# Moving u loads and out stores into SyncE's queue beside the transposes, and reordering the opening of an attention-and-mixer kernel

## The chip, the cores and the metric

One core of a Trainium2 chip. The metric is device time of one execution in microseconds (us), taken as the median of several runs; spans and stage times come from profiled executions. Engines are named as in the profile: PE is TensorE's matmuls, PEld its weight loads, DVE VectorE, ACT ScalarE, POOL GpSimd, SP SyncE. A "q" behind the name is the engine's instruction queue, where loads and stores are issued. Line numbers such as L351 are lines of the kernel in question; the changed kernel's lines are shifted by some 20.

## The reference

```python
batch, seq, d_model, d_qk, rank = 8, 3136, 256, 64, 32
# gated attention unit
scores = (1 / seq) * z @ z.transpose(0, 2, 1)
x = u * (np.maximum(scores, 0) ** 2 @ v)
# mixer: a low-rank mix over the sequence, then an MLP over the channels
h = x.transpose(0, 2, 1) @ U @ V
y = x + h.transpose(0, 2, 1)
out = y + np.maximum(y @ w_ch1, 0) @ w_ch2        # w_ch1: 256 x 1024, w_ch2: 1024 x 256
```

The score matrix is symmetric. The kernel computes, for each of the 25 tiles of 128 rows, only half of the blocks of its row ("A"), and gets the other half by transposing.

## The kernel before

Four things matter here.

First, PE walks through the 25 output tiles of a batch. For an output tile it needs 12 transposed blocks, a "strip", which SyncE makes from A by one DMA transpose. A strip is ordered 4 output tiles before it is needed (`AHEAD = 4`, 5 buffers).

```python
transpose = nc.sync.dma_start_transpose
pool_dma = nc.gpsimd.dma_start

def turn(b, o):                          # SyncE's queue
    strip = strip_pool.tile([P, HALF, P], BF16, name="strip")
    transpose(out=strip, in_=A[o][:, P:])
    strips[b, o] = strip
```

Second, all plain traffic goes through GpSimd's queue: u in, out back, and v, which is cast from fp32 to bf16 on the way. u and out have two buffers each.

```python
def load_v(b, part):
    ...
        pool_dma(out=v_bf[:, t0:t1, :], in_=rows(v[b])[:, t0:t1, :])
...
def load_u(b, o):
    ...
        pool_dma(out=u_sb[:, :n, :], in_=rows(u[b])[:, t0 : t0 + n, :])
...
                store = pool_dma if b + 1 < B else nc.sync.dma_start
                    store(out=rows(out[b])[:, t : t + nk, :], in_=o_sb[:, :nk, :])
```

Third, the MLP of batch b-1 runs in eight "bursts" between the attention of batch b, and each burst emits one of the nine loads of v of batch b+1 (the last burst two):

```python
burst_at = {4: (0, 1), 8: (2, 3), 13: (4, 5), 17: (6, 7)}
...
    loads = [lambda k=k: load_v(b + 1, V_PARTS[k]) for k in ((n,) if n < NC else (n, n + 1))]
    steps = _merge(steps, loads)
```

v has two buffers, so v of batch b+1 can go in as soon as the attention of batch b-1 has ended, which is at the start of batch b. An engine's queue runs in order, and in GpSimd's queue the v loads stand between stores and u loads.

Fourth, the opening: z of batch 0 is loaded in parts, doubled on VectorE, transposed on PE, and the first four output tiles are computed with scores kept in borrowed room, among it the second v buffer (so v of batch 1 can't come early).

```python
load_z(0, parts[:2]); ...               # GpSimd
double_z(0, parts[:2])                   # VectorE
turn_on_pe([(8, 12), (12, 16)], sets[0])
...
rooms = [v_both[1][:, t : t + 4, :] for t in range(0, NF, 4)]
```

## Time and profile before

| | before |
|---|---|
| median of 3 runs | 1019.78 us (1015.84 to 1021.53) |
| span of the profiled run | 1013.1 us |
| PE busy | 990.8 us (98%) |
| idle PE | 22.3 us |

The page's busy lines, its PE rows in 40 slices, and the chain of work that ended last:

```profile
PE 990.8 (98%) x13816; PEld 785.3 (78%) x13856; DVE 541.2 (53%) x977; ACT 613.5 (61%) x834; POOL 172.2 (17%) x318
...
PE   7899999999999999999999999999999999999998
...
PE 89%; DVE 4%; DMA 3%; ACT 2%; issue 1%; POOL 0%; DVEq 0%; POOLq 0%; ACTq 0%
```

PE is the bound and is full everywhere except in the first slices and the last. The busy times by stretch say where the idle time lies; the columns are the stretch, then busy us and number of instructions of PE, PEld, DVE, ACT and POOL, then granted clock, DMA share and GB/s:

```profile
0.00:30.00 30.00, 21.89 (x258) 16.67 (x259) 17.14 (x33) 20.70 (x30) 12.40 (x28) 1.00 0.79 146
30.00:60.00 30.00, 25.22 (x360) 18.88 (x361) 24.24 (x48) 25.57 (x41) 3.68 (x6) 0.94 1.07 177
60.00:130.00 70.00, 69.95 (x1178) 56.58 (x1174) 50.96 (x95) 51.20 (x73) 14.82 (x25) 1.00 1.17 200
130.00:960.00 830.00, 825.30 (x11676) 660.91 (x11709) 429.29 (x772) 490.96 (x663) 140.73 (x258) 1.00 0.91 168
960.00:1013.10 53.10, 48.47 (x350) 32.26 (x354) 19.58 (x31) 25.10 (x30) 0.55 (x1) 1.00 0.32 92
```

From 60 to 960 PE idles 4.75 us in all.

### The profile page before, as it was taken

The numbers are of one execution on the slowest core, as the hardware profiler recorded it, in microseconds if no ns is written. First come the engines' busy times: TensorE is split into PE (matmuls) and PEld (weight loads), VectorE is DVE, ScalarE is ACT, GpSimd is POOL, SyncE is SP. The second block draws the span as 40 slices with busy tenths as digits, with TensorE's granted clock in tenths as the row PEclk, the third lists the DMA queues.
The fourth block names the chain that finished last, engine by engine and source line by source line (L and its number), as shares of the span: only waits on it lengthen the run. The fifth ranks groups of instructions, "written<-read, shape, count | busy, mean of one in ns | idle before, by whom it ended". The sixth has DMA issues, their size and how long they took to land.

```text
span 1013.1 us, 31291 instructions
## 1 busy us (share of the span) xinstructions
PE 990.8 (98%) x13816; PEld 785.3 (78%) x13856; DVE 541.2 (53%) x977; ACT 613.5 (61%) x834; POOL 172.2 (17%) x318
## 2 busy tenths in 40 slices
PE   7899999999999999999999999999999999999998
PEld 5678878787778877788787887878878788787856
DVE  5878654456544665446644556445664356542242
ACT  6887664667646666456764667556674666643154
POOL 4122112121121111221112211112111120011000
PEclk9999999999999999999999999999999999999999
DMA  8999989999999998989989997989979998778432
GB/s 155 154 199 229 170 155 183 187 177 152 164 193 170 176 168 155 190 168 174 167 170 171 181 169 141 193 170 188 157 154 194 176 179 143 143 136 174 104 97 97
DMA packets 414584, 167.70 MB, mean 166 GB/s; under 512 B 389408, under 2 KB 399328, under 8 KB 414448
## 3 DMA queue, kind: packets, MB, share of 16 engines
q1 hardware_dynamic: 384944, 99.16, 60.7%
q0 software_dynamic: 29504, 66.55, 28.5%
q8 instruction: 108, 1.77, 0.7%
q14 instruction: 28, 0.23, 0.1%
HBM read 61.88 MB, written 25.69 MB: 86 GB/s over the span
## 4 chain that ended last, share of the span: by engine, by line
PE 89%; DVE 4%; DMA 3%; ACT 2%; issue 1%; POOL 0%; DVEq 0%; POOLq 0%; ACTq 0%
PE ps L351 47%; PE ps L562 16%; PE ps L520 16%; PE ps L278 7%; ACT A L291 1%; DMA out_dram<-o_sb 1%; PE ps L385 1%; PE ps L442 1%; DVE A L293 1%; DVE x_bf L502 1%; PE ps L488 1%; DVE both L366 1%; DMA strip<-A 1%; DVE x_bf L375 0%; DMA zT<-z_bf 0%
## 5 line engine op out<-in xcount | busy, mean ns | idle before, releaser
L291 ACT ACTIVATE A<-ps 128x832 bf16<-128x832 f32 (+8 forms) x469 | 352.7, 763 | 155.9 <-PE ps L278 146.0
L351 PE MATMUL ps<-v,A 64*128 64x256 bf16 x4864 | 335.6, 271 | 4.9 <-DVE both L366 2.0
L293 DVE TENSOR_TENSOR A<-A 128x832 bf16<-128x832 bf16 (+8 forms) x469 | 240.3, 524 | 145.7 <-ACT A L291 141.9
L351 PE MATMUL ps<-v,strip 64*128 64x256 bf16 x4420 | 306.8, 269 | 1.3 <-DMA strip<-A 1.2
L351 PEld LDWEIGHTS <-A 64*128 64x128 bf16 x4864 | 239.6, 94 | 49.8 <-issue 15.3
L538 ACT ACTIVATE relu_bf<-ps 128x1024 bf16<-128x1024 f32 (+2 forms) x208 | 187.7, 908 | 142.0 <-PE ps L520 140.0
L351 PEld LDWEIGHTS <-strip 64*128 64x128 bf16 x4420 | 221.3, 94 | 35.5 <-DMA strip<-A 1.7
L562 PE MATMUL ps<-w_bf,relu_bf 128*128 128x256 bf16 x1600 | 204.7, 273 | 0.2 <-ACT relu_bf L536 0.2
L573 DVE TENSOR_TENSOR o_sb<-ps,x_bf 128x512 f32<-128x512 f32 (+1 forms) x104 | 69.7, 670 | 250.8 <-PE ps L562 230.7
L520 PE MATMUL ps<-ut,w_bf 128*128 128x512 bf16 (+2 forms) x856 | 197.3, 351 | 2.5 <-ACT relu_bf L538 0.3
L562 PEld LDWEIGHTS <-relu_bf 128*128 128x128 bf16 x1600 | 155.9, 98 | 47.3 <-issue 3.2
L335 POOL DMA_DIRECT2D u_sb<-in_u_dram x96 | 53.6, 559 | 470.6 <-DVE x_bf L375 438.2
L520 PEld LDWEIGHTS <-w_bf 128*128 128x128 bf16 x896 | 85.1, 98 | 61.3 <-issue 6.8
L278 PE MATMUL ps<-zT 64*128 64x416 bf16 (+8 forms) x812 | 130.7, 312 | 0.0
L365 ACT COPY both<-ps 128x512 f32<-128x512 f32 (+1 forms) x104 | 58.8, 567 | 73.6 <-PE ps L351 66.8
L581 POOL DMA_DIRECT2D out_dram<-o_sb x84 | 46.0, 548 | 274.6 <-DVE o_sb L573 270.6
L366 DVE TENSOR_TENSOR both<-ps,both 128x512 f32<-128x512 f32 (+1 forms) x104 | 69.3, 666 | 27.0 <-ACT both L365 26.7
L375 DVE TENSOR_TENSOR x_bf<-both,u_sb 128x512 bf16<-128x512 f32 (+1 forms) x104 | 69.8, 672 | 3.6
L502 DVE TENSOR_TENSOR x_bf<-ps,x_bf 128x512 bf16<-128x512 f32 (+1 forms) x112 | 65.5, 626 | 8.4 <-PE ps L488 8.2
L278 PEld LDWEIGHTS <-zT 64*128 64x128 bf16 x812 | 42.2, 94 | 4.0
L225 POOL DMA_DIRECT2D v<-in_v_dram x61 | 34.4, 567 | 0.2 <-PE ps L520 0.2
L278 PE MATMUL ps<-relu_bf 64*128 64x416 bf16 (+9 forms) x121 | 23.7, 363 | 2.2 <-ACT A L291 1.0
(52 smaller groups left out, 231.6 us busy)
## 6 DMA issues: line engine op xcount, KB each, us to landing
u_sb<-in_u_dram POOLq DMA_DIRECT2D x96, 256.0 KB, 3.7
out_dram<-o_sb POOLq DMA_DIRECT2D x84, 256.0 KB, 3.3
v<-in_v_dram POOLq DMA_DIRECT2D x57, 192.0 KB, 4.5
strip<-A SPq DMA_TRANSPOSE x196, 5.3
out_dram<-o_sb SPq DMA_DIRECT2D x12, 256.0 KB, 2.1
z_c<-in_z_dram POOLq DMA_DIRECT2D x7, 384.0 KB, 6.3
w_bf<-in_moe_w_ch_dram POOLq DMA_DIRECT2D x2, 512.0 KB, 8.3
u_sb<-in_u_dram POOLq DMA_DIRECT2D x16, 64.0 KB, 2.7
```

The costliest lines, as they stand in the source:

```text
L278: mm(out=ps[:, k, :n], lhsT=zT[halves[k], j, :], rhs=zT_flat[halves[k], c : c + n], start=True, stop=True,)
L291: nc.scalar.activation(out=dst, in_=src, func=AF.Relu, scale=sc)
L293: nc.vector.tensor_tensor(out=dst, in0=dst, in1=dst, op=ALU.mult)
L351: mm(out=acc[t0][h][:, (o - t0) * D : (o - t0 + 1) * D], lhsT=w[halves[h]], rhs=v_both[b % 2][halves[h], j, :], start=start, stop=stop, **kw,)
L365: nc.scalar.copy(out=both[:, :w], in_=banks[1][:, :w])
L366: nc.vector.tensor_tensor(out=both[:, :w], in0=banks[0][:, :w], in1=both[:, :w], op=ALU.add)
L375: nc.vector.tensor_tensor(out=x_at(b, t0, n), in0=split(both[:, :w]), in1=u_sb[:, :n, :].rearrange("p t (a c) -> p t a c", c=P), op=ALU.mult,)
L502: nc.vector.tensor_tensor(out=q, in0=split(ps[h][:, : len(ks) * D]), in1=q, op=ALU.add)
L520: mm(out=ps[i][:, :w] if apart else ps[:, i, :w], lhsT=w1_bf[:, db, (hp + i) * P : (hp + i + 1) * P], rhs=uT[c][:, db, len(chunks[c]) * P ...
L538: nc.scalar.activation(out=relus[c][:, hp : hp + 2, :w], in_=ps[:, :, :w], func=AF.Relu)
L562: mm(out=ps[:, k * D : (k + 1) * D], lhsT=relus[c][:, ht, q : q + P], rhs=w2_bf[:, ht, :], start=(ht == 0), stop=(ht == NH - 1),)
L573: nc.vector.tensor_tensor(out=o_sb[:p, :nk, :].rearrange("p t (a c) -> p t a c", c=P), in0=split(ps[:p, : nk * D]), in1=x_at(b, t, nk)[:p] ...
```

## The change

The intent: take the plain traffic away from GpSimd's software queue and put it in one queue with the transposes; start PE warm and z early; bring all first loads (v, z and weights of batches 0 and 1) up front, with the first strip behind them; hide the first pair closings. The diff, cut to its core:

```diff
+    fifo = nc.sync.dma_start
     transpose = nc.sync.dma_start_transpose
...
+    def first_z(parts):
+        ...
+        nc.vector.memset(wide, 0.0)
+        for _ in range(7):                       # warm PE while z lands
+            mm(out=ps[:, 0, :], lhsT=zT_rest[:, 0, :], rhs=wide, start=True, stop=True)
+        for t0, t1 in parts:                     # z as fp32, by SyncE
+            fifo(out=z_f, in_=rows(z[0])[:, t0:t1, :])
+        for (t0, t1), z_f in zip(parts, landed): # doubled by two engines
+            nc.vector.tensor_copy(out=z_bf[:, t0:t1, 0, :], in_=z_f)
+            nc.scalar.copy(out=z_bf[:, t0:t1, 1, :], in_=z_f)
...
-            pool_dma(out=u_sb[:, :n, :], in_=rows(u[b])[:, t0 : t0 + n, :])
+            fifo(out=u_sb[:, :n, :], in_=rows(u[b])[:, t0 : t0 + n, :])
...
-                store = pool_dma if b + 1 < B else nc.sync.dma_start
-                    store(out=rows(out[b])[:, t : t + nk, :], in_=o_sb[:, :nk, :])
+                    fifo(out=rows(out[b])[:, t : t + nk, :], in_=o_sb[:, :nk, :])
...
-        for s in fetches[:3]:
-            s()
+        run(fetches)
+        if B > 1:
+            for part in V_PARTS:
+                load_v(1, part)
...
-        rooms = [v_both[1][:, t : t + 4, :] for t in range(0, NF, 4)]
+        rooms = [A[j % NT][:, : 2 * NG * P] for j in range(LEAD + NG, LEAD + 3 * NG)]
...
+            if i == 4:
+                for o in outs[::2]:
+                    load_u(0, o)
+                if B > 1:
+                    fifo(out=mark, in_=v_both[1][:1, NF, :8])   # SyncE waits for v of batch 1
...
-        for pair in pairs[-2:]:
+        for o in outs[1::2]:                     # finish and close one output pair at a time
             nxt.pop(0)()
-            use(pair)
-        for o in outs[1::2]:
+            for pair in pairs[-2:]:
+                use(pair, (o - 1, o))
             close_pair(0, o)
...
-                if i in v_at:                    # batch 0's steps
-                    load_v(b + 1, v_at[i])
```

More of the change, by code (lines that the diff above doesn't have):

```diff
@@ L198, in turn_z @@
             )
+    def first_z(parts):
+        z_bf = z_tiles[0] = stage.tile([P, NT, 2, dqk], BF16, name="z_bf")
+        wide = zT_rest[:, :4, :].rearrange("p t c -> p (t c)")
+        nc.vector.memset(wide, 0.0)
+        ps = pair_psum()
+        for _ in range(7):
+            mm(out=ps[:, 0, :], lhsT=zT_rest[:, 0, :], rhs=wide, start=True, stop=True)
+        landed = []
+        for t0, t1 in parts:
+            z_f = u_pool.tile([P, 2, D], FP32, name="u_sb").rearrange("p a c -> p (a c)")
+            z_f = z_f.rearrange("p (t c) -> p t c", c=dqk)
+            fifo(out=z_f, in_=rows(z[0])[:, t0:t1, :])
+            landed.append(z_f)
+        for (t0, t1), z_f in zip(parts, landed):
+            nc.vector.tensor_copy(out=z_bf[:, t0:t1, 0, :], in_=z_f)
+            nc.scalar.copy(out=z_bf[:, t0:t1, 1, :], in_=z_f)
     def turn_on_pe(parts, banks):
@@ L210, in turn_on_pe @@
                 )
-            copy = nc.vector.tensor_copy if t0 % 8 else nc.scalar.copy
+            copy = nc.vector.tensor_copy if t0 % 8 or t1 == NF else nc.scalar.copy
             copy(
@@ L334, in load_u @@
         if o < NF:
-            pool_dma(out=u_sb[:, :n, :], in_=rows(u[b])[:, t0 : t0 + n, :])
+            fifo(out=u_sb[:, :n, :], in_=rows(u[b])[:, t0 : t0 + n, :])
         else:
             for r in halves:
-                pool_dma(out=u_sb[r, 0, :], in_=u[b, NF * P :, :])
+                fifo(out=u_sb[r, 0, :], in_=u[b, NF * P :, :])
         u_tiles[b, t0] = u_sb
@@ L578, in step @@
                 )
-                store = pool_dma if b + 1 < B else nc.sync.dma_start
                 if t < NF:
-                    store(out=rows(out[b])[:, t : t + nk, :], in_=o_sb[:, :nk, :])
+                    fifo(out=rows(out[b])[:, t : t + nk, :], in_=o_sb[:, :nk, :])
                 else:
-                    store(out=out[b, NF * P :, :], in_=o_sb[:TAIL, 0, :])
+                    fifo(out=out[b, NF * P :, :], in_=o_sb[:TAIL, 0, :])
         return [
@@ L608, in start_up @@
         parts = ((8, 16), (0, 8), (16, NF))
-        load_z(0, parts[:2])
+        first_z(parts[:2])
         nc.gpsimd.memset(eye, 1.0)
@@ L624, in start_up @@
             load_v(0, part)
-        double_z(0, parts[:2])
         turn_on_pe([(8, 12), (12, 16)], sets[0])
@@ L632, in start_up @@
             open_pair(0, o)
-            load_u(0, o)
         if B > 1:
             load_z(1, WHOLE)
-        for s in fetches[:3]:
-            s()
+        run(fetches)
+        if B > 1:
+            for part in V_PARTS:
+                load_v(1, part)
         nxt = [s for j in range(LEAD, LEAD + NG) for s in turned(0, j)]
-        rooms = [v_both[1][:, t : t + 4, :] for t in range(0, NF, 4)]
-        rooms = [r.rearrange("p (a t) d -> p a (t d)", a=2) for r in rooms]
-        rooms += [x_bf[:, g].rearrange("p (a w) -> p a w", a=2) for g in (2, 3)]
+        rooms = [A[j % NT][:, : 2 * NG * P] for j in range(LEAD + NG, LEAD + 3 * NG)]
+        rooms = [r.rearrange("p (a w) -> p a w", a=2) for r in rooms]
         pairs = [(8, 9), (10, 11), (12, 13), (14, 15), (6, 7), (3, 4), (5,), (1, 2)]
@@ L644, in start_up @@
         where = {}
+        mark = small.tile([P, D], BF16, name="mark", tag="t1_sb")[:1, :8]
         def make(pair):
@@ L658, in make, with use @@
                 score(0, [(j, c0, NG * P, room) for j in pair])
-        seen = []
-        def use(pair):
+        def use(pair, some):
             for j in pair:
-                for o in outs:
+                for o in some:
                     at = (o - FIRST) * P
-                    stop = [o % 2 == 1 and len(seen) == NT - 1 - h for h in range(2)]
+                    stop = [o % 2 == 1 and j == NF - h for h in range(2)]
                     beside(o, j, where[j][:, at : at + P], stop)
-                seen.append(j)
         for i, pair in enumerate(pairs):
+            if i == 4:
[3 more added lines that the diff above has]
+                    fifo(out=mark, in_=v_both[1][:1, NF, :8])
             if i == 3:
@@ L673, in start_up @@
             if i == 5:
-                ps = pair_psum()
-                turn_on_pe([(16, 20), (20, NF)], [ps[:, 0, :], ps[:, 1, :]])
+                turn_on_pe([(16, NF)], [pair_psum().rearrange("p a w -> p (a w)")])
                 turn_on_pe([(NF, NT)], [pair_psum()[:, 0, :]])
@@ L681, in start_up @@
             if i > 1:
-                use(pairs[i - 2])
-        for pair in pairs[-2:]:
+                use(pairs[i - 2], outs)
+        for o in outs[1::2]:
             nxt.pop(0)()
-            use(pair)
-        for o in outs[1::2]:
+            for pair in pairs[-2:]:
+                use(pair, (o - 1, o))
             close_pair(0, o)
@@ L692, in start_up, with use_stored @@
             load_u(0, o)
-        fetches[3]()
-        if B > 1:
-            double_z(1, WHOLE)
-            turn_z(1, WHOLE)
         pairs = [(j, j - 1) for j in range(LEAD - 1, LEAD - FIRST, -2)]
-        def use_stored(js):
+        def use_stored(js, some):
             for j in js:
-                for o in outs:
+                for o in some:
                     if 0 <= o - j <= HALF:
@@ L712, in start_up @@
         nxt += [lambda pair=pair: make_stored(pair) for pair in pairs[:2]]
-        own = [lambda j=j: use_stored([j]) for j in outs]
-        for s in _merge(nxt, own):
-            s()
+        run(nxt[:2])
+        own = [
+            lambda j=j, some=some: use_stored([j], some)
+            for some in (outs[:2], outs[2:])
+            for j in outs
+            if j <= some[-1]
+        ]
+        run(_merge(nxt[2:], own))
         rest = []
@@ L724, in start_up @@
                 more.pop(0)()
-            use_stored(pair)
+            use_stored(pair, outs)
+            if B > 1 and i in (1, 2):
+                part = ((0, FIRST), (FIRST, NF))[i - 1]
+                double_z(1, (part,))
+                turn_z(1, (part,))
             if i == len(pairs) - 1:
@@ L780 @@
         own = own_at if b else first_at
-        v_at = dict(zip((9, 11, 12, 14, 16, 18, 20, 22, 23), V_PARTS)) if b == 0 else {}
         ahead = dict(zip((2, 3, 6, 7, 10, 11, 14), range(NC)))
```

## The prediction

> **What bounds it now.** TensorE. The page gives PE 990.8 of 1013.1 us busy; the chain of work that ended last is 89% PE. PE idles (windows) 8.1 us in 0-30, 4.8 in 30-60, 0.05 in 60-130, 4.7 in all of 130-960, 4.6 in the tail. In the middle it also runs at its rate: the chain shows 24 attention matmuls in 1.31 us (54.6 ns each) in every batch, one batch per 122.3 us. Steady state has under 5 us to give, the tail is hardly touched; the gain must come from the first 60 us.
>
> **What the opening loses (chain, timeline).**
> 1. PE starts at 4.87: z, issued by GpSimd at 1.30, lands at 4.25 and is doubled by VectorE until 4.82.
> 2. PE is cold: from 4.87 to about 14.5, 16 attention matmuls take 1.71 us against 0.87 later. About 8.5 us at half rate lose 4.2. The granted-clock column shows 1.00. The Trainium skill, "TensorE: Matmul & The Clock Gate", Part 1, says an idle array starts at half clock and needs about 3.4 us of sustained work; the trace agrees in the factor, but took 9 us, with gaps inside.
> 3. From 17 to 29 ScalarE (9.8 of 10 us busy in 20-30) paces the scores.
> 4. From 28.9 to 35.1 the pair closings and an early 1.87 us doubling of batch 1's z stand in PE's way: 2.7 us idle, and half rate again (about 1.5 lost).
> 5. At 46.5 PE waits 1.2 us for a strip queued behind a whole-batch z transpose, at 53 another 1.2 for a square.
>
> **The change.** Seven dummy 512-column matmuls (about 3 us cold) run while z lands; z goes as fp32 by SyncE, cast by VectorE and ScalarE in parallel. Real work starts at 4-4.5 us, warm by 5-6. But ScalarE then binds: it has about 17.6 us of work between 7.3 and 29, so that phase ends near 24.5 instead of 29: items 1-3 together give about 4.5 us. Splitting the last uses by output pair hides closings: about 3. Split, later z transposes: about 1. Against it: 2.1 MB more (w2, v of batch 1) go before the first strip. At the early 220 GB/s they end near 28-30 us; the first strip lands near 33-34, when it is needed: a stall of 0-2 us. Opening total: 7-10 us.
>
> Steady state: 110 loads and 90 stores move from GpSimd to SyncE's queue, 0.33-0.55 us of issue each, off the path. One behind a transpose (1.5 us to issue, 5.3 to landing) lands later, but loads have about a pair and a half of slack, stores two buffers. GpSimd, no longer held by stores and u, will issue the next batch's v in one burst; strips are 4 blocks (about 20 us) ahead. I expect -1 to +2 us.
>
> **Prediction: 1010 us, 1003 to 1017 in 8 of 10.** Faster by over 2%: 0.05; within 2%: 0.92; slower: 0.03.
>
> **What would show it.** First transposes on PE at 4-4.5 us; groups of 16 in 0.87 us by 7 us; second group of outputs starting near 25-26 without a half-rate stretch; PE idle in 0-60 cut from 12.9 to 6-8 us; batch period still 122.3; tail unchanged.
>
> **What would make it wrong.** Strips waiting behind the marker for batch 1's v (a PE stall at 30-40); SyncE blocked in order by a u load or store, giving PE waits in every batch (a longer period); or ScalarE not saturating, so that the warm array gains more.

## More of the kernel before

The timeline of GpSimd at the start of batch 2 shows how v loads (L225) stand among u loads (L335) and stores (L581). The bracket is GpSimd's idle time before the instruction and who ended it:

```profile
246.16 0.55 POOL L335 DMA_DIRECT2D u_sb<-in_u_dram  x1 [6.76 <-DVE x_bf L375]
246.70 0.55 POOL L225 DMA_DIRECT2D v<-in_v_dram  x1
255.05 0.55 POOL L581 DMA_DIRECT2D out_dram<-o_sb  x1 [7.79 <-DVE o_sb L573]
255.59 0.56 POOL L225 DMA_DIRECT2D v<-in_v_dram  x1
```

GpSimd idles most of the time, and each v load goes out only when the store or u load ahead of it has been released by VectorE.

## The result, and the profile after

| | before | after |
|---|---|---|
| median, same chip | 1017.81 us (1014.42 to 1021.53, 4 runs) | 1062.83 us (1060.3 to 1067.68, 4 runs) |
| ratio | | 1.0447 (95%: 1.0391 to 1.0503) |
| span of the profiled run | 1013.1 us | 1061.0 us |
| PE busy / idle | 990.8 / 22.3 us | 1006.9 / 54.1 us |

A ratio is the mean time of one kernel's runs over that of the other's of the same rounds, so it is not quite the ratio of the medians quoted. Executions over 1.5% slower than the fastest of the same kernel are left out of the means. The change is 4.5% slower, where I had put 0.03 on "slower".

The same lines of the page after:

```profile
PE 1006.9 (95%) x13823; PEld 788.5 (74%) x13863; DVE 541.6 (51%) x978; ACT 614.2 (58%) x835; POOL 58.2 (5%) x113
...
PE   7799799997999979999999998999989999999998
...
PE 79%; DMA 13%; DVE 4%; ACT 3%; issue 1%; POOL 0%; SPq 0%; DVEq 0%; ACTq 0%; POOLq 0%
```

The PE row has dents at 7 and 8 that come back every five slices, with one of them missing (at half of the span), and DMA has gone from 3% to 13% of the chain. By stretches:

```profile
0.00:30.00 30.00, 23.75 (x289) 16.93 (x290) 19.55 (x36) 23.25 (x34) 16.42 (x35) 1.00 1.04 188
30.00:60.00 30.00, 22.53 (x307) 16.02 (x303) 19.63 (x43) 21.54 (x36) 1.70 (x4) 0.89 1.01 177
60.00:130.00 70.00, 62.63 (x1101) 51.91 (x1097) 45.05 (x85) 44.35 (x65) 5.34 (x10) 0.94 1.10 175
130.00:1000.00 870.00, 841.96 (x11662) 665.59 (x11695) 435.89 (x783) 497.54 (x669) 34.76 (x65) 0.98 0.88 161
1000.00:1061.00 61.00, 56.06 (x486) 38.08 (x485) 21.44 (x34) 27.54 (x34) 0.00 (x0) 1.00 0.30 81
```

To place the loss in time I take one fixed point of each batch: the start of the block for the short last tile (its own line, L385 before, L406 after), which lies in the middle of a batch. The distances between them, read from the PE timelines, in us:

| | start to first | 0 to 1 | 1 to 2 | 2 to 3 | 3 to 4 | 4 to 5 | 5 to 6 | 6 to 7 | to the end |
|---|---|---|---|---|---|---|---|---|---|
| before | 66.4 | 103.2 | 123.6 | 122.4 | 122.6 | 122.2 | 122.4 | 122.2 | 108.0 |
| after | 68.5 | 112.9 | 130.1 | 133.2 | 123.8 | 128.5 | 133.2 | 122.7 | 108.1 |

The opening has lost 2.1 us. The first six distances between batches have lost 45.3 us together. The seventh, 6 to 7, has lost 0.5. That one is a natural experiment: in it u and out run through SyncE's queue as everywhere, but there is no ninth batch whose v could be loaded. (Nor its z and scores; so this stretch alone does not single out v.) One of the six, 3 to 4, has lost only 1.2; it is taken up below.

What stands at the start of each of the six? GpSimd's timeline at the start of batches 1 and 2 (v loads are now L246 and, for the short last tile, L249):

```profile
106.91 4.29 POOL L246 DMA_DIRECT2D v<-in_v_dram  x8 [68.25 <-PE ps L372]
...
115.97 0.52 POOL L249 DMA_DIRECT2D v<-in_v_dram  x1 [1.60 <-DMA v<-in_v_dram]
...
239.18 4.29 POOL L246 DMA_DIRECT2D v<-in_v_dram  x8 [92.21 <-PE ps L372]
```

GpSimd has run ahead to the first v load, waits for PE to finish with the buffer, and then sends everything within 10 us (106.91 to 116.5); before, the loads of one batch went out one by one, the next ones at 275.74 and 282.05. Meanwhile SyncE and PE, start of batch 2:

```profile
237.83 6.34 SPq L334 DMA_TRANSPOSE strip<-A  x2
244.27 0.53 SPq L356 DMA_DIRECT2D u_sb<-in_u_dram  x1
244.91 13.57 SPq L334 DMA_TRANSPOSE strip<-A  x2
```

```profile
250.89 0.60 PE L372 MATMUL ps<-v,strip 64*128 64x256 bf16 x7
256.89 0.39 PE L372 MATMUL ps<-v,strip 64*128 64x256 bf16 x1 [5.41 <-DMA strip<-A]
```

SyncE needs 13.57 us only to issue two strips; PE runs out of them and idles 5.41 us. The chain that ended last names the strip that PE waits for (start, us from its order to its landing):

```profile
239.37 17.48 DMA strip<-A
```

It was ordered 0.19 us after the first v load. It is the strip of the batch's fourth tile, and PE first needs it at the end of the third, because the first tile of a pair also does one matmul for the second (`half(b, o + 1, NF, 1, block(b, o + 1, NF), ...)`). That was at 251.49, when the matmuls before it ended: the lead was 12.1 us. Over a whole batch a tile takes 4.9 us (122.3 us over 25 tiles), but that average includes the MLP. Here no MLP stands between the tiles: the first three begin at 240.20, 244.91 and 247.89, some 3 us each and 1.6 us of the mixer's U. 17.5 us to landing against 12.1 of lead is the whole stall.

The distance 3 to 4 shows how little decides. GpSimd sends its burst there as well, at 502.64, but the strip in the same place had been ordered 0.68 us earlier, at 501.96; it landed in 7.4 us, and PE waited for no strip.

The stretches after the stall of batch 2 show a second cost:

```profile
253.00:256.00 3.00, 0.00 (x0) 0.00 (x0) 0.00 (x0) 0.00 (x0) 0.00 (x0) 0.84 1.11 107
256.00:259.00 3.00, 2.11 (x20) 1.53 (x22) 0.00 (x0) 0.26 (x1) 0.00 (x0) 0.50 1.24 215
259.00:262.00 3.00, 3.00 (x32) 2.13 (x30) 1.89 (x4) 1.46 (x2) 0.00 (x0) 0.53 1.21 225
262.00:265.00 3.00, 3.00 (x56) 2.63 (x52) 1.74 (x3) 2.31 (x4) 0.00 (x0) 1.00 1.01 199
```

After the stall PE works at a granted clock of 0.50 for about 5 us, until 261.85: 32 matmuls in 3 us, then 56. So a stall of 5 us costs about 8 (an estimate: 5.4 idle, and half of the 5 us at half rate). This is why PE's busy time rose by 16.1 us, of which the seven dummy matmuls are only 3.2. The Trainium skill, "TensorE: Matmul & The Clock Gate", Part 1, says that an idle window of about 3.4 us sends the array back to half clock; the trace agrees for this stall (0.84, 0.50, 0.53, 1.00). But less than a whole idle window is enough here: in the same profile the clock also fell right after idle gaps of only 2.33 and 1.94 us, at 644.14 and 770.43. In the clock records of the thirteen profiles it fell 45 times before the last matmuls of a run, and each time PE had been idle for 1.57 us or more of the 3.41 us before. Where the clock stayed full, no stretch between the same marks had more than 1.85 us idle.

The DMA queues over 17 us at the start of batch 2, which comes 12 us earlier in the kernel before: packets, MB, share of 16 engines' time. Before, 228 to 245:

```profile
q1 hardware_dynamic: 5939, 1.49, 72.4%
q0 software_dynamic: 464, 0.93, 28.8%
...
strip<-A SPq DMA_TRANSPOSE x3, 4.6
```

After, 240 to 257:

```profile
q0 software_dynamic: 1308, 1.64, 68.0%
q1 hardware_dynamic: 3464, 1.09, 52.0%
...
strip<-A SPq DMA_TRANSPOSE x3, 15.9
```

q1 is SyncE's queue, q0 GpSimd's. (The last line of each fence is the median time from issue to landing of the strips issued in the window: 4.6 us and 15.9. Over the whole run of the kernel before it is 5.3.) While the burst lasts, SyncE's queue gets through 3464 packets against 5939 before, and some of those are now u's. The Trainium skill, "DMA: Bandwidth & Descriptors", "Issuing engines are not separate DMA queues", says that transfers of all engines run on the same 16 DMA engines and interleave. The trace agrees, with those two packet counts.

### The profile page after: what moved, and what is told of

Read it like the earlier page. It is cut to its first block, busy times and chain, and to the rows that moved or that the text cites. A ratio compares the mean times of both kernels' runs of the same rounds, so it can differ in the third digit from the quotient of the medians.

```text
span 1061.0 us, 31346 instructions
## 1 busy us (share of the span) xinstructions
PE 1006.9 (95%) x13823; PEld 788.5 (74%) x13863; DVE 541.6 (51%) x978; ACT 614.2 (58%) x835; POOL 58.2 (5%) x113
## 4 chain that ended last, share of the span: by engine, by line
PE 79%; DMA 13%; DVE 4%; ACT 3%; issue 1%; POOL 0%; SPq 0%; DVEq 0%; ACTq 0%; POOLq 0%
PE ps L372 39%; PE ps L583 17%; PE ps L541 16%; DMA strip<-A 10%; PE ps L299 5%; ACT A L312 2%; DVE A L314 1%; DMA zT<-z_bf 1%; DVE x_bf L523 1%; PE ps L406 1%; PE ps L509 1%; DMA z_c<-in_z_dram 1%; DMA ut<-x_bf 1%; DVE both L387 1%; DVE x_bf L396 1%
## 5 line engine op out<-in xcount | busy, mean ns | idle before, releaser
L312 ACT ACTIVATE A<-ps 128x832 bf16<-128x832 f32 (+8 forms) x477 | 359.4, 768 | 202.2 <-PE ps L299 190.6
L372 PE MATMUL ps<-v,A 64*128 64x256 bf16 x4988 | 349.7, 272 | 2.4 <-DVE A L314 2.3
L372 PE MATMUL ps<-v,strip 64*128 64x256 bf16 x4420 | 316.3, 273 | 35.0 <-DMA strip<-A 30.3
L314 DVE TENSOR_TENSOR A<-A 128x832 bf16<-128x832 bf16 (+8 forms) x477 | 245.1, 527 | 197.1 <-ACT A L312 194.2
L372 PEld LDWEIGHTS <-A 64*128 64x128 bf16 x4988 | 249.3, 95 | 49.2 <-issue 10.0
L372 PEld LDWEIGHTS <-strip 64*128 64x128 bf16 x4420 | 224.8, 95 | 76.5 <-DMA strip<-A 33.8
L541 PE MATMUL ps<-ut,w_bf 128*128 128x512 bf16 (+2 forms) x856 | 199.7, 355 | 5.0 <-DMA ut<-x_bf 2.2
L299 PE MATMUL ps<-zT 64*128 64x416 bf16 (+8 forms) x812 | 135.0, 316 | 0.0
L246 POOL DMA_DIRECT2D v<-in_v_dram x61 | 32.9, 566 | 536.0 <-PE ps L372 530.6
L509 PE MATMUL ps<-t_sb,V_bf 64*128 64x256 bf16 x200 | 24.4, 285 | 1.6 <-DVE x_bf L523 1.6
L549 DVE TENSOR_SCALAR relu_bf<-ps 128x512 bf16<-128x512 f32 x16 | 11.0, 690 | 15.5 <-PE ps L541 15.5
```

The lines of the kernel that those rows point to most:

```text
L299: mm(out=ps[:, k, :n], lhsT=zT[halves[k], j, :], rhs=zT_flat[halves[k], c : c + n], start=True, stop=True,)
L312: nc.scalar.activation(out=dst, in_=src, func=AF.Relu, scale=sc)
L314: nc.vector.tensor_tensor(out=dst, in0=dst, in1=dst, op=ALU.mult)
L372: mm(out=acc[t0][h][:, (o - t0) * D : (o - t0 + 1) * D], lhsT=w[halves[h]], rhs=v_both[b % 2][halves[h], j, :], start=start, stop=stop, **kw,)
L541: mm(out=ps[i][:, :w] if apart else ps[:, i, :w], lhsT=w1_bf[:, db, (hp + i) * P : (hp + i + 1) * P], rhs=uT[c][:, db, len(chunks[c]) * P ...
```

## The experiments

Theory A: the v loads of the next batch, no longer held back by stores and u loads in GpSimd's queue, go out in one burst and crowd out the strips. Rival B: SyncE's queue, which now holds u loads and stores too, is blocked in order by them, or u and out slow the strips down on the shared queue. For the opening: the marker, the flood of early loads, or a bound elsewhere.

| run | what | median us (ratio to before, 95%) | first point | six distances 0 to 6 |
|---|---|---|---|---|
| before | | 1017.81 | 66.4 | 103.2 123.6 122.4 122.6 122.2 122.4 |
| after | | 1062.83 (1.0447; 1.0391 to 1.0503) | 68.5 | 112.9 130.1 133.2 123.8 128.5 133.2 |
| e1_paced | after, v held back | 1025.34 (1.0052; 0.9982 to 1.0123) | 68.8 | 104.7 124.5 123.3 122.6 124.8 124.4 |
| e2_burst | before, v in a burst | 1114.34 (1.0912; 1.0819 to 1.1005) | 65.6 | 116.1 140.4 139.8 136.0 143.2 140.0 |
| e3_open | after, u and out on GpSimd | 1019.37 (1.0005; 0.9904 to 1.0106) | 68.1 | 105.0 122.2 123.0 122.7 123.5 122.2 |
| e4_nomark | after, no marker | 1064.79 (1.0356; 1.0225 to 1.0487) | 67.8 | 112.0 129.4 133.8 126.4 131.8 127.2 |
| e5_late_paced | e1, v of batch 1 late | 1013.5 (0.9983; 0.9953 to 1.0012) | 61.5 | 104.1 122.8 123.4 122.8 123.1 122.3 |
| e6_late_pool | e5 with u and out on GpSimd | 1013.84 (0.9987; 0.9939 to 1.0035) | 62.3 | 103.7 122.2 124.7 124.4 124.3 122.2 |
| e7_cold | e5, one dummy matmul | 1015.45 (0.9999; 0.9967 to 1.003) | 61.6 | 104.0 122.8 123.4 122.5 122.8 123.1 |
| e8_zfirst | e5, z's last part earlier | 1014.51 (0.9982; 0.9951 to 1.0012) | 59.7 | 104.5 122.4 123.4 123.7 124.5 123.0 |
| e9_small | after, v in shorter runs | 1062.58 (1.047; 1.041 to 1.053) | 68.4 | 114.5 131.2 133.6 128.6 132.5 130.2 |
| e10_threes | e1, v in three bursts | 1028.99 (1.0142; 1.009 to 1.0193) | 67.6 | 104.6 125.5 124.9 123.1 124.6 124.4 |
| e11_best | e6 with e8's order | 1014.84 (1.0007; 0.9949 to 1.0064) | 59.4 | 107.9 122.2 123.2 122.6 122.9 122.7 |

All gave correct results. The kernel before, run beside them, had medians of 1021.67 (e1 to e4), 1015.86 (e5 to e8) and 1013.13 (e9 to e11), so the ratios are to be compared, not the medians. The points and distances are each of one profiled run.

### e1_paced: the burst taken away, SyncE's queue kept

```diff
+    def paced_v(b, k, n):
+        src = relus[min(n, NC - 1)]
+        nc.gpsimd.tensor_copy(out=gate[:1, :], in_=src[:1, 0, :8])
+        load_v(b, V_PARTS[k])
...
-    loads = [lambda k=k: load_v(b + 1, V_PARTS[k]) for k in ...]
+    loads = [lambda k=k, n=n: paced_v(b + 1, k, n) for k in ...]
```

> The changed kernel, with one tiny GpSimd copy (8 values of the ReLU tile that ScalarE has just written) ahead of each v load of batches 2 to 7, so that GpSimd issues them about one per burst of the MLP, as it did before the change; u loads and stores stay in SyncE's queue. Theory A (the nine v loads that GpSimd, no longer held by stores and u loads, issues at once at each batch start crowd out the strip transposes): the batch period goes back from 124-134 to 122.3 us, the strip waits after 60 us vanish, time about 1018 us (1014 to 1022), what remains of the loss being the opening. Theory B (SyncE's queue is blocked in order, a transpose standing behind a u load or store that waits or moves): the stalls stay, 1050 to 1065 us.

Measured: ratio 1.0052 against the changed kernel's 1.0447. PE's waits from 60 us on, as who waited for whom, total us, times, longest:

```profile
PE ps L406 <- DVE x_bf L523: 4.3, 6, 1.7
PE ps L509 <- DVE x_bf L523: 1.6, 9, 0.3
PE ps L372 <- DVE o_sb L594: 0.4, 1, 0.4
PE ps L541 <- ACT relu_bf L559: 0.3, 1, 0.3
```

No wait for a strip is left, with u and out in SyncE's queue just as in the changed kernel. A holds in kind; the time is 3 us over the range that I had given it. B, which wanted 1050 or more, falls. The period did not come back quite: three distances are 124.4 to 124.8. The profile shows most of what is left: at two of the fixed points, 173.58 and 668.74, PE waits 1.66 and 1.51 us for VectorE (the first line above), and after each the clock is 0.50 for 3.41 us. Why VectorE is late there was not looked into.

### e2_burst: the burst alone, on the kernel before

```diff
+                if b and i == 0:
+                    for part in V_PARTS:
+                        load_v(b + 1, part)
...
-    loads = [...]
-    steps = _merge(steps, loads)
```

> The kernel before, with one thing of the change imitated: all nine v loads of the next batch are emitted together at the start of each batch from the second on; u loads and stores stay in GpSimd's queue, the opening is the old one. Theory A: the batch period rises from 122.3 to about 130 us in batches 1 to 6 and the time to 1045-1065 us, with strip waits of 5 to 7 us just after each batch start. Theory B: no change beyond 3 us, about 1018.

Measured: 1114.34 us, beyond the range of A in its own direction: twice the loss of the changed kernel. PE's waits from 60 us on:

```profile
PE ps L351 <- DMA strip<-A: 59.7, 11, 10.4
PE ps L520 <- DMA ut<-x_bf: 12.8, 6, 3.6
```

So the burst needs nothing else of the change to do harm. Why more than in the changed kernel? In GpSimd's order u and z now stand behind the burst, and perhaps prolong it: at the start of batch 2, u goes out at 247.70 and z at 253.40, right behind v, and z takes 17.1 us to land. That batch shows a second stall, of 8.8 us, which ends at 272.4. That z and u are what makes it worse was not tested by itself.

### e3_open: u and out back on GpSimd, the new opening kept

```diff
+        load = fifo if b == 0 and place(o) <= 2 * NG else pool_dma
-            fifo(out=u_sb[:, :n, :], ...)
+            load(out=u_sb[:, :n, :], ...)
...
+                store = pool_dma if b + 1 < B else fifo
-                    fifo(out=rows(out[b])[...], in_=...)
+                    store(out=rows(out[b])[...], in_=...)
```

> The changed kernel with u loads (after the opening) and out stores (except the last batch's) put back into GpSimd's queue; the opening is the new one, and v loads stand again behind stores in GpSimd's order. Both theories expect the batch period back at 122.3 us and about 1018 us; A says it lands within 2 us of e1_paced, because the queue of u and out is worth nothing by itself; B says it is 30 us or more faster than e1_paced.

Measured: ratio 1.0005, periods back at 122.2 to 123.5. Nothing here holds v back but stores and u loads in the same queue, as before the change. The difference to e1_paced, 0.5% by the ratios, is within both intervals; e5 and e6 repeat that comparison below.

### e4_nomark: the marker

```diff
-                if B > 1:
-                    fifo(out=mark, in_=v_both[1][:1, NF, :8])
```

> The changed kernel without the tiny marker load that holds SyncE until v of batch 1 has landed. If the marker causes the 4.5 us strip wait at 37.5 to 42 us and the half-rate stretch after it, 4 to 6 us faster than the changed kernel (about 1058). If the early flood of loads itself is the cause (strips then crawl among the v loads), no more than 2 us faster, with the first strips taking 12 us or more to land. The later stalls stay in either case.

Measured: 1064.79 us. Two of its four runs counted as slow, and they pull this median up; the two fast ones were 1050.46 and 1060.99, a ratio of 1.0356 against the changed kernel's 1.0447, with intervals that overlap. So the time leaves a small gain open, and the profile has to answer. In the changed kernel the marker went out at 35.20, when v of batch 1 had landed; the first strip was issued at 36.09, and PE stood still from 37.5 to 41.96. Without the marker SyncE starts the strips at 23.44, but they crawl (the second number is the time that issuing the two took):

```profile
23.44 14.61 SPq L334 DMA_TRANSPOSE strip<-A  x2
```

The wait of 4.5 us becomes waits of 1.45 and 2.29 us, and the first point moves only from 68.5 to 67.8. In this profile the marker did not make the loss of the opening; it chose where to take it. The flood ahead of the strips is the cause, the same collision as in the batches.

### e5_late_paced: the flood taken away as well

```diff
-        if B > 1:
-            for part in V_PARTS:
-                load_v(1, part)
...
+                if b == 0 and i in v_at:             # the steps of the kernel before
+                    hold(x_at(0, turns(i - 2))[:1, 0, 0, :8])
+                    load_v(1, v_at[i])
```

> e1_paced, and v of batch 1 no longer loaded in the opening: its nine loads go back to the steps of batch 0 where the kernel before has them, each behind a tiny GpSimd copy of a value that a pair closing has just written (so that GpSimd cannot run ahead); the marker is gone, u and out stay in SyncE's queue. If the early flood is what eats the gain of the warm, better ordered opening, the first strips land before they are needed, the last-tile block of batch 0 starts at 60 to 63 us instead of 68, and the time is 1010 to 1015 us, 0.5 to 1% under before. If the opening is bound elsewhere (ScalarE, the late third part of z), that block stays at 66 to 68 and the time at 1018 to 1022.

Measured: the first point moves from 68.8 (e1) to 61.5, which is 4.9 us ahead of the kernel before. So the new opening does gain once the loads are out of its way. The time, though, is 0.9983 of before, and the interval includes 1. Adding up the distances of batches 0 to 7, e5 has 841.0 us against before's 838.7: about half of what the opening gained is lost again later in this profile.

### e6_late_pool: which queue, once v is paced

Its edit is e3's, with e5's opening and without the tiny copies.

> The same opening as e5_late_paced, but u loads (after the opening) and out stores in GpSimd's queue again, which then paces the v loads by itself; no tiny copies. If the queue move is worth nothing by itself, within 3 us of e5_late_paced, with a batch period of 122.2 to 122.5 in both. If u and out in SyncE's queue cost something (e1_paced had three batch periods of 124.5 to 124.8 against 122.2 to 123.5 in e3_open), 4 us or more faster than e5_late_paced.

Measured: 1013.84 against 1013.5, ratios 0.9987 and 0.9983. The move of u and out into SyncE's queue, which was the headline of the change, is worth nothing that can be measured here (0.04%, with intervals of 0.3 and 0.5% to either side) as soon as v does not come in a burst.

### e7_cold: without the warm-up

```diff
-        for _ in range(7):
+        for _ in range(1):
```

> e5_late_paced with one dummy matmul instead of seven. If the warm-up is worth what I predicted (4 us at half rate, less what ScalarE's pace hides): 2 to 4 us slower than e5_late_paced, attention groups of 16 at 1.7 us until about 12 us. If ScalarE hides all of it: within 1 us.

Measured: the first point at 61.6 against 61.5, times alike within their intervals. Seven dummies are worth no more than one here, and the profile has a reason that I had not foreseen: in e5's own profile the warm-up did not hold. So this run does not tell what a warm-up that holds is worth. Attention groups of 16 matmuls in e5 (seven dummies):

```profile
1.26 3.17 PE L209 MATMUL ps<-zT 128*128 128x512 bf16 x7 [1.26 <-DVE zT L206]
...
8.18 1.80 PE L372 MATMUL ps<-v,A 64*128 64x256 bf16 x16 [0.28 <-DMA v<-in_v_dram]
10.16 1.82 PE L372 MATMUL ps<-v,A 64*128 64x256 bf16 x16
```

The same group takes 1.05 us from 7.86 on in the changed kernel's profile, 1.80 and 1.82 here, with the same seven dummies. Between the dummies and the first group PE has one gap of 0.96 us in the changed kernel, and three of 0.34, 0.96 and 0.28 us in e5. The Trainium skill, "TensorE: Matmul & The Clock Gate", Part 1, says that the window of the activity monitor runs freely and that the number of cold matmuls varies from run to run. In e5 all three gaps, 1.58 us together, lie in the 3.41 us before the clock fell at 8.31, about as much as the least that went before any fall; one gap of 0.96 is less than that. Neither the gaps nor the phase of the window was varied by itself.

### e8_zfirst: z's third part ahead of v

```diff
-        load_v(0, (12, 18))
         load_z(0, parts[2:])
+        load_v(0, (12, 18))
```

> e5_late_paced with the third part of batch 0's z loaded ahead of v tiles 12 to 17, because in the changed kernel it took 8.2 us to land and PE waited 1.6 us for its doubling at 11.3 to 12.9. If that wait lies on the critical path: 1 to 2 us faster than e5_late_paced; if v tiles 12 to 17 then come late instead, no gain.

Measured: the first point 1.8 us earlier, at 59.7, as hoped. The time is not (0.9982 against 0.9983), since in its profile the seven distances from the first point to batch 7's are 845.0 us, 4.0 longer than in e5.

### e9_small: the same burst in shorter runs

For the large v loads of batches 1 to 7:

```diff
-            pool_dma(out=v_bf[:, t0:t1, :], in_=rows(v[b])[:, t0:t1, :])
+            at = t0 // 6 * 6 + t0 // 3 % 2
+            pool_dma(out=v_bf[:, at : at + 5 : 2, :], in_=rows(v[b])[:, at : at + 5 : 2, :])
```

> The changed kernel, burst and marker kept, but each of the eight large v loads of batches 1 to 7 takes every second tile of six instead of three adjoining ones: the same nine loads, bytes and issue times, in runs of 256 instead of 768 values, so three times as many v packets of a third of the size. In the changed kernel's burst from 110 to 127 us GpSimd's packets took 157 ns each (72.3% of 16 engines over 17 us, 1254 packets) against 68 ns for SyncE's (53.4%, 2147), which outside the burst take about 27 to 30. If the engines take turns packet by packet, short v packets let the transposes through about twice as fast: strips land in 8 to 12 us instead of 16 to 19, the time falls to 1025-1048 us. If only the bytes in flight count, nothing is gained: 1055 to 1070.

Measured: 1062.58 us, no gain. A miss of mine about the mechanism. The queues from 110 to 127 us, first the changed kernel:

```profile
q0 software_dynamic: 1254, 1.58, 72.3%
q1 hardware_dynamic: 2147, 0.75, 53.4%
```

and e9_small:

```profile
q0 software_dynamic: 2651, 1.31, 82.5%
q1 hardware_dynamic: 3141, 1.02, 65.5%
```

SyncE's queue did get 46% more packets through (3141 over 2147), but v landed no sooner (16.9 us against 16.2), and neither did the strips: at the starts of batches 1 and 2 they took 16.4 and 14.5 us (medians), against 10.7 and 15.9 in the changed kernel. How the DMA engines share themselves out between the two queues stays open; what is settled is that the burst is long enough, and the strips slow enough within it, at either packet size.

### e10_threes: three bursts of three

```diff
+        if k % 3 == 0:                    # the tiny copy ahead of every third load only
             nc.gpsimd.tensor_copy(out=gate[:1, :], in_=src[:1, 0, :8])
```

> e1_paced with a tiny copy ahead of every third v load only, so that v comes in three bursts of three loads. If strips are late because the whole burst has to pass (4 blocks, some 20 us, of lead are used up by it), a third of it is absorbed by the lead: within 5 us of e1_paced, 1020 to 1028 us. If any burst stalls the strips in proportion to its bytes, the loss remains: 1045 us or more.

Measured: 1028.99, ratio 1.0142 against 1.0052 of e1; its intervals overlap slightly, and the time is 1 us over the range that I gave. In the window of its first group of three, from 125 to 142 us, three v loads land in 8.7 us and strips in 7.7 us (median), and from 60 us on PE waits for no strip. So a lead of four tiles absorbs a third of the burst there, as A says. But the groups of three also come at another place than the whole burst: at 128, 158 and 206 us, beside the MLP, where a tile lasts longer than at the start of a batch. Whether the smaller burst or the later place saved the strips was not separated, here or in e1.

### e11_best: the best parts together

> Candidate to beat both: the opening of e8_zfirst (z's third part ahead of v tiles 12 to 17, no early v of batch 1, no marker) with u and out in GpSimd's queue as in e6_late_pool. The last-tile block of batch 0 starts at about 60 us (before: 66.4) and the batch period is 122.3 to 123: about 1010 us, 0.6% under before (0.3 to 0.9%). If what the opening gains is lost again in the batches, as in e5 and e8, within 0.3% of before.

Measured: ratio 1.0007, no gain. The first point is at 59.4, 7 us ahead of before, and the next distance is 107.9 instead of 103.2: PE waits there three times for ScalarE (1.08, 0.28 and 1.37 us between 70 and 90 us), and ScalarE itself waits, 8.6 us from 60 to 170, for strips to have been read out of A. The gain of the opening is mostly handed back in batch 0, where the DMA engines are the fullest (share 1.25 from 73 to 93 us). No run beats the kernel before clear of noise.

## Why the prediction was wrong

**What bounds the kernel; where a gain can lie.** Right. PE, with under 5 us idle in the batches.

**The opening: "7-10 us".** Wrong, in two terms. Some parts on the engines went about as foretold: first transposes at 4.27 us (foretold 4 to 4.5), full-speed groups at 7.86 (by 7), and no half-rate stretch around the closings. The first failed term is the pace of the scores: the first outputs were to be done near 24.5 us and the second to start at 25 to 26. By the count of their 196 matmuls the second outputs start at 27.59, against 30.24 before, and their first full group of 16 at 31.78 against 35.92: 2.7 to 4.1 us ahead, where items 1 to 3 and the closings were to give about 7.5. One wait that the sum does not have is 1.57 us for the third part of z, until 12.89; the rest was not looked into. The second failed term is "a stall of 0-2 us" for the strip behind the marker. I expected the early loads to end near 28-30 us and the first strip to be there at 33-34. They ended at 35.2, and PE idled until 41.96: 4.5 us, and about 5 us of half rate after it. PE's idle time from 0 to 60 us was 13.7 us, foretold 6 to 8. The rate of 220 GB/s was too high (188 in the first 30 us). With the flood removed (e5) the opening gains 4.9 us, still under my 7.

**The warm-up.** I claimed no separate gain for it, since ScalarE would bind; e7 shows 0. But I did assume that it would hold, and in e5's profile it did not.

**"u loads and stores ... off the path".** Right: e5 and e6 differ by 0.04%, and batch 7 shows 122.7 us against 122.2.

**"GpSimd ... will issue the next batch's v in one burst; strips are 4 blocks (about 20 us) ahead. I expect -1 to +2 us."** This is the step that failed. The event was foretold and its size was not: 45.3 us over six batch starts. I set a lead, 20 us, against a latency, 5.3 us to landing, and both were wrong at the place where they met. The latency I took for a constant; in the burst the strip that PE waited for took 17.5 us. The lead of 20 us is four times the average tile of 4.9 us, but the burst comes at the start of a batch, where no MLP stands between the tiles, and this strip is needed already in the tile before its own: there the lead was 12.1 us (239.37 to 251.49), and the difference is the stall. By these figures a true lead of 20 us would have covered that strip (an estimate; no run has it). I also left out the clock: after the two longest stalls, 7.4 and 5.4 us, PE worked for another 5 us or so at half rate. And the loss is no constant either: 1.2 us at one batch start, 6.3 to 10.8 at the others.

**What would make it wrong.** I named three things: the strips behind the marker (it happened, 4.5 us), SyncE blocked in order by u or stores (e1 refutes it), and an unsaturated ScalarE (no). The thing that happened, 45 us of it, was in none of them.

## What to carry to other kernels

Before moving an instruction out of an in-order queue, ask what stood behind it: its waits may have been the only pacing of the rest, and idle time of an engine that costs nothing can still be doing this work. Where bulk prefetches share the DMA engines with transfers that the bound engine waits for, hold them back explicitly, by a dependence on work of the step at which they are wanted. Measure a prefetch lead in us at the very place where the collision falls, not by the average tile, and compare it with the latency under that collision, not with the median one.

## What the Trainium skill lacked or had wrong

- "DMA: Bandwidth & Descriptors", "Issuing engines are not separate DMA queues", says that issuing from several engines only saves the sequencer's time to start a transfer. It lacks the pacing that comes with a queue: the same nine v loads, freed from the stores ahead of them, cost 45.3 us here, and the burst alone 9% (e2_burst).
- The same page has no landing time for a transpose beside a burst of casting loads. Here it is 15.9 us (median at the start of batch 2) against 4.6 in the same stretch before, and the issue itself stretches: two transposes held SyncE's queue for 13.57 us.
- The same page, "Queues, rings and completion order", says that a DMA engine takes turns between queues packet by packet. Its packets may hold several descriptors, so they need not be the packets that the profile counts, and the runs neither confirm nor refute it: with v in runs a third as long (e9_small), SyncE's queue passed 3141 packets in 17 us instead of 2147, and the time stayed the same.
- "TensorE: Matmul & The Clock Gate" advises warming up with at least 4 us of matmuls before measuring. About 3 us of dummies before real work, with gaps of up to 0.96 us after them (one in the first profile, three in the second), gave a warm array in one profile (16 matmuls in 1.05 us) and a cold one in another (1.80), and no measurable time in the end (e7_cold). No page says how much idle time within a window lets the clock fall: in the 45 falls of these profiles it was 1.57 us or more of 3.41.
